# Decode attention with FFN, two layers: score sums moved from VectorE to TensorE, wide V matmuls, layers interleaved by batch row

## The chip, the cores and the metric

The kernel runs on one core of one Trainium2 chip. The metric is device time in microseconds, taken over repeated runs. The granted TensorE clock is given as a share of full speed. "MB" is 10^6 bytes, except that a "2 MB tile" is 2048 KB (2.097 MB).

## The reference

Eight batch rows, one new token each, go twice through the same attention block (32 heads of 128, a cache of 4096 keys and values per head, D = 640) and the same FFN (640 to 1728 to 640). All data is bf16.

```python
x = A_x                                   # (8, 1, 640)
for _ in range(2):                        # written out twice in the original
    x = x + _A_ref(_layernorm(x), A_k_cache, A_v_cache, A_wq, A_wo)
    x = x + _B_ref(_layernorm(x), B_w1, B_w2)

# _A_ref: q = x @ wq
#         p = softmax(q . k * 128**-0.5) over 4096 keys, o = p . v per head, then o @ wo
# _B_ref: relu(x @ w1) @ w2
```

Both layers read the whole K and V cache: 2 x (268 + 268) MB. With one query per row and head, each K or V element is used once per layer, so the run is mostly the reading of 1.07 GB.

## The kernel before

A block is one batch row and eight heads. The order of blocks is by head range, then by batch row. K comes in 2 MB tiles (two heads, 32 keys of each head per partition), four buffers deep. V comes in 1 MB tiles, eight deep. The scores are made on VectorE (DVE): one multiply with the query, four halving adds, one reduce.

```python
blocks = [(b, *r) for r in ranges for b in range(B)]       # ranges of 8 heads
...
# k_phase, per two heads
nc.sync.dma_start(
    out=K_sb.rearrange("p (h j) d -> p h j d", h=HK),
    in_=A_k_cache[b, h : h + HK].rearrange("h (p j) d -> p h j d", p=P),
)
...
nc.vector.tensor_tensor(out=K4, in0=K4, in1=qap, op=ALU.mult)          # 128 x 8192
w = Dh
for _ in range(TL):                                                    # TL = 4
    w //= 2
    nc.vector.tensor_tensor(
        out=K_sb[:, :, 0:w], in0=K_sb[:, :, 0:w], in1=K_sb[:, :, w : 2 * w], op=ALU.add
    )
nc.vector.tensor_reduce(out=S_sb[:, hl0 : hl0 + HK, :], in_=K_sb[:, :, 0:RW], axis=AX.X, op=ALU.add)
...
# v_phase, per head: 32 matmuls with a one-column stationary operand
for j in range(J):
    nc.tensor.matmul(
        o_ps[0:1, hb * Dh : (hb + 1) * Dh], lhsT=P_sb[:, hl, j : j + 1],
        rhs=V_sb[:, j, :], start=(j == 0), stop=(j == J - 1),
    )
...
drive([k_phase(bi), s_phase(bi - 1), v_phase(bi - 2)])     # a pipeline over blocks
...
attention_layer(0, pre0)       # all rows
pre1 = attention_prealloc(1)   # wq is loaded a second time
ffn_layer(0)
attention_layer(1, pre1)
ffn_layer(1)
```

Of the kernel before, what the change touches and what calls it, by code (L numbers as in the profile page):

```python
# [12 lines left out]
ALU = mybir.AluOpType  # L13
AX = mybir.AxisListType


def _bcast_ap(ap: bass.AP, shape_strides) -> bass.AP:
    return bass.AP(
        tensor=ap.tensor,
        offset=ap.offset,  # L20
        ap=[list(ap.ap[0])] + [[int(st), int(n)] for (st, n) in shape_strides],
    )


KERNEL_OPTS = dict(
    k_bufs=4,
    v_bufs=8,
    tree_levels=4,
    heads_per_block=8,
    edge_heads=0,  # L30
    heads_per_ktile=2,
    merged_mult=True,
)
# [3 lines left out]
def kernel(  # L37
# [12 lines left out]
    opts = dict(KERNEL_OPTS)  # L50
# [7 lines left out]
    assert Sq == 1 and Dh == P and HD == H * Dh  # L58
    assert D % P == 0 and Sk % P == 0 and HD % 512 == 0 and B <= P
    DC = D // P  # L60
    J = Sk // P
    NQ = HD // 512
# [3 lines left out]
    NCH = 2 if D > 512 else 1  # L66
    assert D % NCH == 0 and D // NCH <= 512
    DN = D // NCH
    inv_sqrt_dh = 1.0 / float(np.sqrt(Dh))
    eps = 1e-5  # L70
    TL = opts["tree_levels"]
    assert Dh % (1 << TL) == 0
    RW = Dh >> TL
    HK = opts["heads_per_ktile"]

    HPB = min(opts["heads_per_block"], H)
    assert H % HPB == 0
    ranges = [(h, HPB) for h in range(0, H, HPB)]
    blocks = [(b, *r) for r in ranges for b in range(B)]
    EH = opts["edge_heads"]  # L80
    if EH and EH < HPB and HPB % EH == 0:
        b0, h00, nh00 = blocks[0]
        bl, h0l, nhl = blocks[-1]
        first = [(b0, h00 + k, EH) for k in range(0, nh00, EH)]
        last = [(bl, h0l + k, EH) for k in range(0, nhl, EH)]
        blocks = first + blocks[1:-1] + last
    for (_, _, nh) in blocks:
        assert nh % HK == 0
    NBLK = len(blocks)
    MAXNH = max(nh for (_, _, nh) in blocks)  # L90
    HB = 4
    while any(nh % HB for (_, _, nh) in blocks):
        HB //= 2
    _done = {r: 0 for r in ranges}
    range_done_at = {}
    for bi, (b, h0, nh) in enumerate(blocks):
        for r in ranges:
            if r[0] <= h0 and h0 + nh <= r[0] + r[1]:
                _done[r] += nh
                if _done[r] == B * r[1]:  # L100
                    range_done_at[bi] = r
    completion_order = [range_done_at[bi] for bi in sorted(range_done_at)]
    assert len(completion_order) == len(ranges)

    x_flat = A_x.rearrange("b s d -> (b s) d")
    out_flat = out.rearrange("b s d -> (b s) d")
# [3 lines left out]
    state = ctx.enter_context(tc.tile_pool(name="state", bufs=1))  # L110
    psum_g = ctx.enter_context(tc.tile_pool(name="psum_g", bufs=1, space=bass.MemoryType.PSUM))

    sel = consts.tile([B, B, P], BF16, name="sel")
    nc.gpsimd.memset(sel, 0.0)
    nc.gpsimd.affine_select(
        out=sel, in_=sel, pattern=[[-1, B], [0, P]], compare_op=ALU.not_equal,
        fill=1.0, base=0, channel_multiplier=1,
    )
    ident = consts.tile([B, B], BF16, name="ident")
    nc.gpsimd.memset(ident, 0.0)  # L120
    nc.gpsimd.affine_select(
        out=ident, in_=ident, pattern=[[-1, B]], compare_op=ALU.not_equal,
        fill=1.0, base=0, channel_multiplier=1,
    )
    one_bf = consts.tile([1, 1], BF16, name="one_bf")
    nc.vector.memset(one_bf, 1.0)
    ones_f = consts.tile([P, P], FP32, name="ones_f")
    nc.vector.memset(ones_f, 1.0)
# [5 lines left out]
    )  # L134
    eps_c = consts.tile([P, 1], FP32, name="eps_c")
    nc.vector.memset(eps_c, eps)

    x_bf = state.tile([B, D], BF16, name="x_bf")
    nc.sync.dma_start(out=x_bf, in_=x_flat)
    x_sb = state.tile([B, D], FP32, name="x_sb")  # L140
    nc.vector.tensor_copy(out=x_sb, in_=x_bf)

    w1_sb = wres.tile([P, DC, Dff], BF16, name="w1_sb")
    w2_sb = wres.tile([P, FC, D], BF16, name="w2_sb")

    def load_ffn_weights():
        nc.sync.dma_start(out=w1_sb, in_=B_w1.rearrange("(c p) f -> p c f", p=P))
        if n_full > 0:
            nc.sync.dma_start(
                out=w2_sb[:, :n_full, :],  # L150
                in_=B_w2[0 : n_full * P, :].rearrange("(c p) n -> p c n", p=P),
            )
        if Dff % P != 0:
            rem = Dff % P
            nc.sync.dma_start(out=w2_sb[:rem, n_full, :], in_=B_w2[n_full * P : Dff, :])

    def layernorm_T(psum_pool, out_pool):
        lnes = ExitStack()
        work = lnes.enter_context(tc.tile_pool(name="lnwork", bufs=1))
        ssum = work.tile([B, 1], FP32, name="ln_ssum")  # L160
        nc.vector.tensor_reduce(out=ssum, in_=x_sb, axis=AX.X, op=ALU.add)
        mean = work.tile([B, 1], FP32, name="ln_mean")
        nc.vector.tensor_scalar(out=mean, in0=ssum, scalar1=1.0 / D, scalar2=None, op0=ALU.mult)
        xc = work.tile([B, D], FP32, name="ln_xc")
        nc.vector.tensor_scalar(out=xc, in0=x_sb, scalar1=mean, scalar2=None, op0=ALU.subtract)
        sqj = work.tile([B, D], FP32, name="ln_sqj")
        var = work.tile([B, 1], FP32, name="ln_var")
        nc.vector.tensor_tensor_reduce(
            out=sqj, in0=xc, in1=xc, scale=1.0 / D, scalar=0.0, op0=ALU.mult, op1=ALU.add, accum_out=var
        )  # L170
        std = work.tile([B, 1], FP32, name="ln_std")
        nc.scalar.activation(out=std, in_=var, func=ACT.Sqrt, bias=eps_c[:B, :], scale=1.0)
        rstd = work.tile([B, 1], FP32, name="ln_rstd")
        nc.vector.reciprocal(out=rstd, in_=std)
        xln = work.tile([B, D], BF16, name="ln_xln")
        nc.vector.tensor_scalar(out=xln, in0=xc, scalar1=rstd, scalar2=None, op0=ALU.mult)
        xT_ps = psum_pool.tile([P, DC, B], BF16, name="xT_ps", bufs=1)
        for c in range(DC):
            nc.tensor.transpose(out=xT_ps[:, c, :], in_=xln[:, c * P : (c + 1) * P], identity=ident[:, :])
        xlnT = out_pool.tile([P, DC, B], BF16, name="ln_xlnT")  # L180
        nc.vector.tensor_copy(out=xlnT, in_=xT_ps)
        lnes.close()
        return xlnT

    def add_psum_to_x(y_list):
        for n in range(NCH):
            nc.vector.tensor_tensor(
                out=x_sb[:, n * DN : (n + 1) * DN], in0=x_sb[:, n * DN : (n + 1) * DN],
                in1=y_list[n], op=ALU.add,
            )  # L190

    def attention_prealloc(li: int):
        axs = ExitStack()
        qpool = axs.enter_context(tc.tile_pool(name=f"qpool{li}", bufs=1))
        q_sb = qpool.tile([B, HD], BF16, name="q_sb")
        oT_sb = qpool.tile([P, H, B], BF16, name="oT_sb")
        wq_es = ExitStack()
        wq_pool = wq_es.enter_context(tc.tile_pool(name=f"wq_pool{li}", bufs=1))
        wq_sb = wq_pool.tile([P, DC, HD], BF16, name="wq_sb")
        nc.sync.dma_start(out=wq_sb, in_=A_wq.rearrange("(c p) n -> p c n", p=P))  # L200
        return dict(axs=axs, qpool=qpool, q_sb=q_sb, oT_sb=oT_sb, wq_es=wq_es, wq_sb=wq_sb)

    def attention_layer(li: int, pre):
        axs = pre["axs"]
        qpool = pre["qpool"]
        q_sb = pre["q_sb"]
        oT_sb = pre["oT_sb"]
        wq_sb = pre["wq_sb"]

        with ExitStack() as es:  # L210
            psum_q = es.enter_context(tc.tile_pool(name=f"psum_q{li}", bufs=2, space=bass.MemoryType.PSUM))
            xlnT = layernorm_T(psum_q, qpool)
            for n in range(NQ):
                q_ps = psum_q.tile([B, 512], FP32, name="q_ps")
                for c in range(DC):
                    nc.tensor.matmul(  # L216
                        q_ps, lhsT=xlnT[:, c, :], rhs=wq_sb[:, c, n * 512 : (n + 1) * 512],
                        start=(c == 0), stop=(c == DC - 1),
                    )
                nc.scalar.copy(out=q_sb[:, n * 512 : (n + 1) * 512], in_=q_ps)  # L220
        pre["wq_es"].close()

        wo_pool = axs.enter_context(tc.tile_pool(name=f"wo_pool{li}", bufs=1))
        kv_es = ExitStack()
# [241 lines left out]
```

## Time and profile before

| | before |
|---|---|
| time, median | 2803 us |
| DVE / PE busy share | 91% / 55% |
| load queue, share of 16 engines' time | 95.2% |
| bytes on the load queue | 1099 MB |
| rate in full stretches | 420 to 421 GB/s |

The lines below are from the page of the kernel before. PE is TensorE, PEld its weight loads, DVE is VectorE, ACT ScalarE, POOL GpSimd, and SP the engine whose queue issues the loads; L267 is line 267 of the kernel. The first line gives busy microseconds of each engine. The next three cut the span into 40 slices (the granted clock in tenths, the DMA busy share in tenths, the rate). The q1 line gives packets, MB and share of the load queue. Then comes the chain of work that ended last, by engine, and last three of the costliest groups (count, busy us, mean ns, idle before).

```profile
...
PE 1545.5 (55%) x17768; PEld 1377.1 (49%) x17768; DVE 2536.3 (91%) x1905; ACT 338.8 (12%) x1433; POOL 3.1 (0%) x10
...
PEclk7676776876777777777867676777777777767778
DMA  8899997999899998999988999899998999989996
GB/s 349 351 417 421 421 404 311 421 421 420 368 405 421 421 420 350 420 421 420 376 340 341 375 420 421 345 374 420 421 420 349 421 420 421 421 352 421 420 421 256
...
q1 hardware_dynamic: 155440, 1099.21, 95.2%
...
DVE 85%; DMA 7%; PE 6%; issue 1%; ACT 1%; SPq 0%; ACTq 0%; DVEq 0%
...
L337 PE MATMUL o_ps<-V_sb,P_sb 128*1 128x128 bf16 x16384 | 1321.2, 257 | 548.0 <-DMA V_sb<-in_A_v_cache_dram 543.0
...
L267 DVE TENSOR_TENSOR K_sb<-K_sb,qb_sb 128x8192 bf16<-128x8192 bf16 x256 | 1129.9, 4414 | 93.7 <-DMA K_sb<-in_A_k_cache_dram 93.4
L277 DVE TENSOR_TENSOR K_sb<-K_sb 128x512 bf16<-128x512 bf16 (+3 forms) x1024 | 1176.8, 1154 | 26.5
...
```

DVE is nearly full, and the chain is 85% DVE. But the queue's packets already take 95.2% of the DMA engines' time. The second view shows why: the windows of the kernel before. The columns are busy us and instruction counts by engine, then the granted clock, the DMA share, and the rate.

```profile
...
core 0: us, PE busy (x) PEld busy (x) DVE busy (x) ACT busy (x) POOL busy (x), PEclk, DMA share, GB/s
140.00:400.00 260.00, 134.34 (x1650) 119.73 (x1650) 253.39 (x191) 33.94 (x152) 0.00 (x0) 0.69 1.01 420
1450.00:1500.00 50.00, 19.55 (x271) 17.50 (x271) 50.00 (x33) 6.40 (x23) 0.00 (x0) 0.65 0.73 286
2600.00:2700.00 100.00, 54.03 (x648) 50.82 (x648) 97.46 (x71) 9.61 (x43) 0.00 (x0) 0.76 1.01 421
2780.00:2800.00 20.00, 11.01 (x118) 6.32 (x115) 5.90 (x15) 1.58 (x2) 0.00 (x0) 0.74 0.01 1
...
```

In undisturbed stretches the DMA share is 1.01 at 420 to 421 GB/s. The rate is lower in the first 140 us, around the layer boundary (286) and in the tail (almost none), and also at six other places: the slices of 311, 368, 350, 345, 349 and 352 in the page's GB/s line. The buffer of wo holds one range of eight heads, and its reload (L370) waits until the projection of that range has read the old piece; every K and V load behind it in the queue waits too. The first line below shows the stretch around one such place, the second the queue's waits at L370 (us in total, times, longest; L299 is TensorE's next matmul after that projection):

```profile
...
400.00:500.00 100.00, 59.12 (x668) 52.52 (x666) 88.96 (x65) 10.69 (x45) 0.00 (x0) 0.71 0.81 333
...
SPq L370 <- PE misc_ps L299: 191.8, 6, 32.0
...
```

In this trace nothing is issued from 404.5 to 436.3 us, and from 420 to 430 us the traffic is zero while DVE is busy for 9.83 of 10 us. Counted against 421 GB/s in 10 us windows, the six places lose 88 us together.

### The profile page before, as it was taken

How to read it: one execution, taken by the hardware profiler on the slowest of the kernel's cores; microseconds unless marked ns; L12 is line 12 of the kernel's file. 1: busy time of each engine (PE TensorE's matmuls, PEld its weight loads, DVE VectorE, ACT ScalarE, POOL GpSimd, SP SyncE). 2: the span in 40 equal slices, each digit the busy share in tenths (PEclk: the TensorE clock that was granted, in tenths of full speed). 3: DMA queues.
4: the chain of work that ended last, by engine and by line, in shares of the span. 5: the costliest groups of instructions: out<-in, count | busy, mean ns of one | idle time of the engine just before them, and what ended most of it. 6: DMA issues, size and time to landing. Idle time of an engine off the chain costs nothing.

```text
span 2800.5 us, 40467 instructions
## 1 busy us (share of the span) xinstructions
PE 1545.5 (55%) x17768; PEld 1377.1 (49%) x17768; DVE 2536.3 (91%) x1905; ACT 338.8 (12%) x1433; POOL 3.1 (0%) x10
## 2 busy tenths in 40 slices
PE   2454455556555555555725454465555555555657
PEld 0354454555545555555614454455554555555546
DVE  5999998999989998999469999989999899989993
ACT  1111111011011111111111111111011011111011
POOL 0000000000000000000000000000000000000000
PEclk7676776876777777777867676777777777767778
DMA  8899997999899998999988999899998999989996
GB/s 349 351 417 421 421 404 311 421 421 420 368 405 421 421 420 350 420 421 420 376 340 341 375 420 421 345 374 420 421 420 349 421 420 421 421 352 421 420 421 256
DMA packets 155617, 1101.80 MB, mean 393 GB/s; under 512 B 12512, under 2 KB 22448, under 8 KB 23088
## 3 DMA queue, kind: packets, MB, share of 16 engines
q1 hardware_dynamic: 155440, 1099.21, 95.2%
q8 instruction: 139, 2.28, 0.3%
q14 instruction: 38, 0.31, 0.0%
HBM read 1099.15 MB, written 0.01 MB: 392 GB/s over the span
## 4 chain that ended last, share of the span: by engine, by line
DVE 85%; DMA 7%; PE 6%; issue 1%; ACT 1%; SPq 0%; ACTq 0%; DVEq 0%
DVE K_sb L277 39%; DVE K_sb L267 37%; DMA K_sb<-in_A_k_cache_dram 7%; DVE S_sb L281 5%; PE o_ps L337 2%; PE y_ps L362 1%; DVE mrow L296 1%; PE q_ps L216 1%; PE misc_ps L299 1%; DVE hmx L302 1%; DMA wq_sb<-in_A_wq_dram 1%; PE y_ps L420 0%; ACT P_sb L314 0%; DVE invL L352 0%; DVE diag L304 0%
## 5 line engine op out<-in xcount | busy, mean ns | idle before, releaser
L337 PE MATMUL o_ps<-V_sb,P_sb 128*1 128x128 bf16 x16384 | 1321.2, 257 | 548.0 <-DMA V_sb<-in_A_v_cache_dram 543.0
L337 PEld LDWEIGHTS <-P_sb 128*1 128x1 bf16 x16384 | 1250.2, 101 | 590.5 <-issue 550.8
L267 DVE TENSOR_TENSOR K_sb<-K_sb,qb_sb 128x8192 bf16<-128x8192 bf16 x256 | 1129.9, 4414 | 93.7 <-DMA K_sb<-in_A_k_cache_dram 93.4
L277 DVE TENSOR_TENSOR K_sb<-K_sb 128x512 bf16<-128x512 bf16 (+3 forms) x1024 | 1176.8, 1154 | 26.5
L251 ACT CAST qb_sb<-bc_ps 128x512 bf16<-128x512 f32 x128 | 68.7, 588 | 1172.4 <-DVE K_sb L267 1171.3
L281 DVE TENSOR_REDUCE S_sb<-K_sb 128x64 f32<-128x512 bf16 x256 | 175.1, 684 | 7.6
L343 ACT CAST o_sb<-o_ps 1x512 bf16<-1x512 f32 x128 | 73.4, 573 | 727.5 <-PE o_ps L337 727.4
L314 ACT ACTIVATE P_sb<-S_sb,nmax 128x32 bf16<-128x32 f32 x512 | 157.0, 308 | 2.0
L346 PE MATMUL oT_ps<-one_bf,o_sb 1*128 1x1 bf16 x512 | 32.1, 163 | 212.9 <-ACT o_sb L343 209.2
L346 PEld LDWEIGHTS <-o_sb 1*128 1x128 bf16 x512 | 21.1, 94 | 237.0 <-ACT o_sb L343 226.5
L319 PE MATMUL misc_ps<-lrow,ones_f 128*128 128x8 f32 x128 | 38.1, 371 | 161.8 <-ACT P_sb L314 161.8
L319 PEld LDWEIGHTS misc_ps<-lrow,ones_f 128*128 128x128 f32 x128 | 32.0, 310 | 171.3 <-ACT P_sb L314 170.6
L299 PE MATMUL misc_ps<-ident_f,mrow 128*8 128x128 f32 x64 | 22.2, 348 | 157.9 <-DVE mrow L296 157.9
L299 PEld LDWEIGHTS misc_ps<-ident_f,mrow 128*8 128x8 f32 x64 | 5.3, 83 | 194.7 <-DVE mrow L296 177.8
L247 PE MATMUL bc_ps<-q_sb,sel 8*128 8x512 bf16 x128 | 49.8, 462 | 91.7 <-ACT qb_sb L251 89.6
L314 ACT ACTIVATION_READ_ACCUMULATOR P_sb<-S_sb,nmax 128x1 f32 x512 | 95.5, 187 | 0.0
L310 ACT ACTIVATE nmax<-misc_ps 128x8 f32<-128x8 f32 x64 | 11.4, 178 | 446.3 <-PE misc_ps L308 446.3
L353 DVE TENSOR_TENSOR oT_sb<-oT_ps,invL 128x8 bf16<-128x8 f32 x64 | 11.9, 185 | 54.9 <-PE oT_ps L346 54.9
L308 PE MATMUL misc_ps<-diag,ones_f 8*128 8x8 f32 x128 | 34.4, 339 | 42.9 <-DVE diag L304 42.9
L308 PEld LDWEIGHTS misc_ps<-diag,ones_f 8*128 8x128 f32 x128 | 28.4, 274 | 58.5 <-DVE diag L304 57.2
L247 PEld LDWEIGHTS <-sel 8*128 8x128 bf16 x128 | 8.9, 99 | 96.3 <-issue 92.7
L302 DVE TENSOR_REDUCE hmx<-misc_ps 8x1 f32<-8x128 f32 x64 | 17.8, 278 | 37.1 <-PE misc_ps L299 37.0
(44 smaller groups left out, 201.9 us busy)
## 6 DMA issues: line engine op xcount, KB each, us to landing
K_sb<-in_A_k_cache_dram SPq DMA_DIRECT2D x256, 2048.0 KB, 27.0
V_sb<-in_A_v_cache_dram SPq DMA_DIRECT2D x512, 1024.0 KB, 24.8
wq_sb<-in_A_wq_dram SPq DMA_DIRECT2D x2, 5120.0 KB, 16.0
wo_sb<-in_A_wo_dram SPq DMA_DIRECT2D x8, 1280.0 KB, 6.2
w_sb<-in_B_w_dram SPq DMA_DIRECT2D x1, 2160.0 KB, 19.8
w_sb<-in_B_w_dram SPq DMA_DIRECT2D x1, 2080.0 KB, 25.0
w_sb<-in_B_w_dram SPq DMA_DIRECT2D x1, 80.0 KB, 23.5
x_bf<-in_A_x_dram SPq DMA_DIRECT2D x1, 10.0 KB
```

Source lines behind the costliest of these rows:

```text
L247: nc.tensor.matmul(bc_ps[:, :gw], lhsT=sel[:, b, :], rhs=q_sb[:, h0 * Dh + g : h0 * Dh + g + gw], start=True, stop=True,)
L251: nc.scalar.copy(out=qb_sb[:, g : g + gw], in_=bc_ps[:, :gw])
L267: nc.vector.tensor_tensor(out=K4, in0=K4, in1=qap, op=ALU.mult)
L277: nc.vector.tensor_tensor(out=K_sb[:, :, 0:w], in0=K_sb[:, :, 0:w], in1=K_sb[:, :, w : 2 * w], op=ALU.add)
L281: nc.vector.tensor_reduce(out=S_sb[:, hl0 : hl0 + HK, :], in_=K_sb[:, :, 0:RW], axis=AX.X, op=ALU.add)
L299: nc.tensor.transpose(out=mT_ps, in_=mrow[:, :nh], identity=ident_f)
L308: nc.tensor.matmul(gmax_ps, lhsT=ones_f[:nh, :], rhs=diag[:nh, :nh], start=True, stop=True)
L314: nc.scalar.activation(out=P_sb[:, hl, :], in_=S_sb[:, hl, :], func=ACT.Exp, bias=nmax[:, hl : hl + 1], scale=inv_sqrt_dh, accum_out=lrow[ ...
L319: nc.tensor.matmul(L_ps, lhsT=ones_f, rhs=lrow[:, :nh], start=True, stop=True)
L337: nc.tensor.matmul(o_ps[0:1, hb * Dh : (hb + 1) * Dh], lhsT=P_sb[:, hl, j : j + 1], rhs=V_sb[:, j, :], start=(j == 0), stop=(j == J - 1),)
L343: nc.scalar.copy(out=o_sb, in_=o_ps)
L346: nc.tensor.matmul(oT_ps[:, hh : hh + 1], lhsT=o_sb[0:1, kk * Dh : (kk + 1) * Dh], rhs=one_bf[0:1, 0:1], start=True, stop=True,)
```

## The change

The intent is to take the halving adds off DVE, to make TensorE cheap enough to take them, and then to keep the load queue full.

- A visit is one batch row and two heads. Heads sit on the two halves of the partitions, 64 keys per partition, so K and V rows are 16 KB per partition in one 2 MB load (8 KB per head before).
- DVE multiplies a tile in two halves. TensorE sums them with 16 identity matmuls of 512 columns into PSUM, the memory that matmuls accumulate in ("fold"), and DVE reduces the last 8.
- Attention uses 16 matmuls per visit of eight columns by 512, at four column positions.
- Rows are visited so that layer 1 of row b runs between parts of layer 0 of row b+1. One V tile per row is kept from layer 0 to layer 1, which saves eight loads of 2 MB. wq is loaded once. So is wo, in four pieces that stay; before, the pieces replaced each other and were read again for layer 1.
- The FFN of one row is sliced over several visits. K and V have two buffers each, and the order on each engine is fixed by hand.

The diff, cut to its core (cuts are marked by ...):

```diff
-                w = Dh
-                for _ in range(TL):
-                    w //= 2
-                    nc.vector.tensor_tensor(
-                        out=K_sb[:, :, 0:w], in0=K_sb[:, :, 0:w], in1=K_sb[:, :, w : 2 * w], op=ALU.add
-                    )
...
+    def pair_src(cache, b, hp):
+        return cache[b, 2 * hp : 2 * hp + 2].rearrange("h (pp j) d -> (h pp) j d", pp=HP)
...
+    def fold(i, part):
+        if part == 0:
+            s_tiles[i] = ps.tile([P, J, RW], FP32, name="s_ps", bufs=2)
+        n = DW // RW
+        for k in range(n):
+            lo = part * DW + k * RW
+            nc.tensor.matmul(
+                s_tiles[i], lhsT=ident_b, rhs=K_tiles[i][:, :, lo : lo + RW],
+                start=(part == 0 and k == 0), stop=(part == 1 and k == n - 1),
+            )
...
+            nc.tensor.matmul(
+                o_ps[32 * c : 32 * c + 8, :], lhsT=P2[k % 2][:, j, 4 * g : 4 * g + 4, :],
+                rhs=V[:, 4 * g : 4 * g + 4, :], start=(g < 4), stop=(g >= n - 4), tile_position=(0, 32 * c),
+            )
...
+        if hp == keep:
+            if layer == 1:
+                V_tiles[v] = kept.pop(b)
+                return
+            V_tiles[v] = kept[b] = rpool.tile([P, J, Dh], BF16, name="V_keep")
...
+            if new:
+                mult(i, 0)
+                fold(i, 0)
+            if 1 <= i <= NV:
+                reduce_s(i - 1)
+            ... (softmax_a, softmax_d, scale_o, add_y of earlier visits)
+            if new:
+                mult(i, 1)
+                fold(i, 1)
+                if i + 2 < NV:
+                    load_k(i + 2)
+            ... (softmax_b, attend, load_v(v + 2), softmax_c, gather_o, project_o)
```

## The prediction

> **What bounds the kernel now.** Two resources are almost equally full. The chain of waits is 85% DVE: per 2 MB K tile one 128x8192 multiply (4.41 us), four halving adds (2.28, 1.22, 0.69, 0.42) and a 0.68 us reduce, 9.7 us x 256 = 2487 of 2536 us busy (groups). But the page's queue lines give the load queue 95.2% of 16 engines' time. By stretches (windows), 140-400 and 2600-2700 us run at 420 to 421 GB/s, DMA share 1.01; nothing runs faster. 1099 MB at 421 GB/s is 2611 us. It is lower only where stalled: 0-30 (334 GB/s), 400-500 (333), 1450-1500 after the layer boundary (286), and a tail (2780-2800) with almost no traffic.
>
> **What the change does.** (a) The DVE keeps the multiply, as two 128x4096 halves (2.28 us each in this trace); the adds become 16 accumulating identity matmuls of 512 columns and one 0.68 us reduce. DVE work per 2 MB pair falls from 9.7 to about 5.3 us, plus some 0.8 us of small operations: about 6.1 x 256 = 1560 us, estimate. (b) The 16384 one-column V matmuls become 4096 eight-column, 512-wide ones at four column positions of the array. (c) The layers are interleaved by batch row, with FFN work sliced between, so there is no boundary stall. (d) wq is read once, and eight 2 MB V tiles are kept for layer 1: 22 MB less, leaving 1072 MB by the shapes. (e) K buffering shrinks to two 2 MB tiles and V to two.
>
> **How much counts.** Nearly 1000 us leaves the DVE, but the DMA floor moves only from 2611 to 1072/421 = 2546 us. Per K+V visit (4.19 MB) the DMA needs 9.97 us. DVE needs 6.1. PE: the 512-column projections started 0.43 us apart at first and about 0.215 later (timeline), so the folds cost 3.4 (warm) to 6.9 us (cold). Column positions should overlap; the Trainium skill, TensorE: Matmul & The Clock Gate, Part 3, states 2.38x for three column tiles, which no run here shows. With that, attention is about 1.2 to 2.5 us, small matmuls about 1.5, giving 6 to 10 us. So DMA binds if PE stays mostly warm.
>
> Does double buffering feed it? A K buffer is held about 2.3 + 1.5 + 2.3 + 1.7 to 3.4 = 8 to 9.5 us of a 20 us turn, leaving over 10 us for 5 us of transfer and its queue. The even visits' softmax chain (fold, maximum, four 0.5 us exponentials, 0.57 us copy, gather, projection, next add) is 8.5 to 10 us: near the period: small leaks, not a new bound.
>
> Sum: 2546 + about 8 head + 20 tail (last V, attention, one FFN row, output) + 25 leaks = **2600 us**, 8 in 10 within **2570 to 2700**. Chances: faster by over 2% 0.93, within 2% 0.06, slower 0.01.
>
> **What would show it.** DVE share falls to about 60%; the queue share rises to 97% or more and GB/s stands at 415 to 421 in nearly all slices, no dip mid-way; the chain turns from DVE to DMA (K tile landings); DVE's main wait is for K loads; o_ps matmuls overlap; PEclk stays about 0.7 or more.
>
> **What would make it wrong.** Column positions that do not overlap, strided 8-element moving reads that run slow in the folds, or a half-rate clock: PE then needs over 10 us a visit, the chain turns to PE, and the time is 2700 to 2900. Or the two-buffer loads arriving too late: DMA idles, slices at 390 to 405 GB/s, 2650 to 2750.

## The result, and the profile after

The changed kernel takes 2582 us (median of 8 runs, 2578 to 2585), the kernel before 2803 us. The ratio is 0.921, 95% interval 0.920 to 0.922. All ratios here are the mean time of one kernel's fast runs over that of the other's in the same rounds, so they are not quite the ratios of the quoted medians.

| | before | after |
|---|---|---|
| time, median | 2803 us | 2582 us |
| DVE / PE busy share | 91% / 55% | 57% / 75% |
| load queue share | 95.2% | 98.7% |
| bytes on the load queue | 1099 MB | 1072 MB |
| rate in full stretches | 420 to 421 GB/s | 426 to 427 GB/s |
| mean granted clock | 0.724 | 0.838 |

The same kinds of lines of the page of the changed kernel, with its line of DMA packets (count, MB, mean rate, and how many packets are small):

```profile
...
PE 1948.9 (75%) x15662; PEld 883.6 (34%) x15662; DVE 1461.2 (57%) x1943; ACT 513.0 (20%) x1604; POOL 2.1 (0%) x15
...
PEclk8778888888888888888888888888888787888887
DMA  9999999999999999999999999999999999999997
GB/s 385 418 414 426 410 409 426 426 426 426 406 427 426 426 424 408 426 425 403 400 425 426 427 419 410 427 426 426 410 417 426 427 413 419 413 426 424 406 426 300
DMA packets 81968, 1074.24 MB, mean 416 GB/s; under 512 B 8256, under 2 KB 14096, under 8 KB 17296
...
q1 hardware_dynamic: 81808, 1071.93, 98.7%
...
DMA 48%; PE 31%; DVE 16%; ACT 4%; issue 1%; DVEq 0%; SPq 0%; ACTq 0%
...
L302 DVE TENSOR_TENSOR K_sb<-K_sb,qb 128x4096 bf16<-128x4096 bf16 x512 | 1171.2, 2288 | 1017.8 <-DMA K_sb<-in_A_k_cache_dram 1017.8
L312 PE MATMUL s_ps<-K_sb,ident_b 128*128 128x512 bf16 x4096 | 1260.5, 466 | 389.8 <-DVE K_sb L302 388.8
...
```

DVE fell from 2536 to 1461 us busy, and its waits for K loads are now 1018 us, the idle time shown in the group of the multiply. The queue's share rose to 98.7%. The chain's largest engine is now DMA, but only 48%: most of the rest (multiply and fold, 14% and 25% of the span in the page's list by line) is the work between a K tile's landing and the request for the next one. No load waits for a wo buffer any more.

The windows of the changed kernel (columns as above), at a visit whose V tile is kept and at the end:

```profile
...
core 0: us, PE busy (x) PEld busy (x) DVE busy (x) ACT busy (x) POOL busy (x), PEclk, DMA share, GB/s
640.00:650.00 10.00, 5.98 (x62) 2.92 (x63) 5.47 (x7) 1.13 (x2) 0.00 (x0) 0.99 1.00 424
650.00:660.00 10.00, 8.18 (x37) 3.11 (x37) 6.16 (x9) 1.95 (x10) 0.00 (x0) 0.66 0.78 300
660.00:670.00 10.00, 8.97 (x81) 4.21 (x82) 8.17 (x12) 1.73 (x3) 0.00 (x0) 1.00 0.99 424
2560.00:2570.00 10.00, 5.50 (x80) 2.36 (x77) 0.98 (x7) 2.46 (x3) 0.00 (x0) 0.50 0.43 179
2570.00:2580.00 10.00, 6.30 (x146) 5.97 (x147) 1.05 (x7) 1.98 (x5) 0.00 (x0) 0.50 0.01 2
...
```

About two thirds of the 10 us windows of the run stand at 424 GB/s or more. At 650 us the rate drops to 300, and such a drop returns about every 32 visits. That is where one V tile is not loaded. The tail of some 20 us has no traffic.

The timeline of TensorE in the changed kernel (start, length, line, operation, count):

```profile
...
start us, us, engine line op out<-in xcount [idle before <-releaser]
...
1209.48 1.04 PE L372 MATMUL o_ps<-V_sb,P 128*8 128x512 bf16 x16
...
```

Sixteen attention matmuls of 512 columns end 1.04 us after they began.

The loss can be counted: for each 10 us window, the shortfall against 427 GB/s. It sums to 68 us: 4 in the first ten, 19 in the tail, and the remaining 45 in between. Of these 45, some 20 lie at the eight visits whose V tile is kept, and some 14 in windows that hold a slice of the FFN (its matmuls are at L191 and L210). Without any shortfall the 1074 MB of all queues would take 2516 us.

### The profile page after: what moved, and what is told of

Read it like the earlier page. It is cut to its first block, busy times and chain, and to the rows that moved or that the text cites. A ratio compares the mean times of both kernels' runs of the same rounds, so it can differ in the third digit from the quotient of the medians.

```text
span 2583.5 us, 36163 instructions
## 1 busy us (share of the span) xinstructions
PE 1948.9 (75%) x15662; PEld 883.6 (34%) x15662; DVE 1461.2 (57%) x1943; ACT 513.0 (20%) x1604; POOL 2.1 (0%) x15
## 3 DMA queue, kind: packets, MB, share of 16 engines
q1 hardware_dynamic: 81808, 1071.93, 98.7%
## 4 chain that ended last, share of the span: by engine, by line
DMA 48%; PE 31%; DVE 16%; ACT 4%; issue 1%; DVEq 0%; SPq 0%; ACTq 0%
DMA K_sb<-in_A_k_cache_dram 47%; PE s_ps L312 25%; DVE K_sb L302 14%; ACT P L349 2%; PE q_ps L287 1%; PE ch_ps L210 1%; PE o_ps L372 1%; DVE S_sb L323 1%; ACT o_sb L377 1%; PE ch_ps L191 1%; PE blk_ps L342 1%; ACT L167 0%; DMA K_sb<-in_A_v_cache_dram 0%; PE blk_ps L329 0%; ACT L165 0%
## 5 line engine op out<-in xcount | busy, mean ns | idle before, releaser
L302 DVE TENSOR_TENSOR K_sb<-K_sb,qb 128x4096 bf16<-128x4096 bf16 x512 | 1171.2, 2288 | 1017.8 <-DMA K_sb<-in_A_k_cache_dram 1017.8
L312 PE MATMUL s_ps<-K_sb,ident_b 128*128 128x512 bf16 x4096 | 1260.5, 466 | 389.8 <-DVE K_sb L302 388.8
L312 PEld LDWEIGHTS <-ident_b 128*128 128x128 bf16 x4096 | 457.5, 114 | 1071.4 <-issue 779.0
L377 ACT CAST o_sb<-o_ps 104x512 bf16<-104x512 f32 x256 | 150.1, 586 | 824.9 <-PE o_ps L372 821.8
L372 PE MATMUL o_ps<-V_sb,P 128*8 128x512 bf16 x3808 | 249.2, 382 | 0.0
L349 ACT ACTIVATE P<-S_sb,nmax 64x64 bf16<-64x64 f32 x512 | 186.8, 365 | 9.0
L323 DVE TENSOR_REDUCE S_sb<-s_ps 128x64 f32<-128x512 f32 x256 | 175.1, 684 | 2.7 <-PE s_ps L312 2.7
L396 PE MATMUL y_ps<-oT,wo_sb 128*128 128x1 bf16 x2560 | 99.7, 163 | 0.3 <-DVE oT L388 0.3
L349 ACT ACTIVATION_READ_ACCUMULATOR P<-S_sb,nmax 64x1 f32 x512 | 94.5, 185 | 0.0
L396 PEld LDWEIGHTS <-wo_sb 128*128 128x128 bf16 x2560 | 82.6, 96 | 0.4 <-DVE oT L388 0.4
```

The source lines that it names most:

```text
L302: nc.vector.tensor_tensor(out=kk, in0=kk, in1=_free(qb_tiles[i][:, lo : lo + DW], [(0, J), (1, DW)]), op=ALU.mult)
L312: nc.tensor.matmul(s_tiles[i], lhsT=ident_b, rhs=K_tiles[i][:, :, lo : lo + RW], start=(part == 0 and k == 0), stop=(part == 1 and k == n ...
L323: nc.vector.tensor_reduce(out=S_tiles[k][:, j, :], in_=s_tiles.pop(i), axis=AX.X, op=ALU.add)
L349: nc.scalar.activation(out=P2[k % 2][r, j, :, hh], in_=S[r, j, :], func=ACT.Exp, bias=nmax[r, j : j + 1], scale=inv_sqrt_dh, accum_out=lro ...
L372: nc.tensor.matmul(o_ps[32 * c : 32 * c + 8, :], lhsT=P2[k % 2][:, j, 4 * g : 4 * g + 4, :], rhs=V[:, 4 * g : 4 * g + 4, :], start=(g < 4) ...
L377: nc.scalar.copy(out=o_sb, in_=o_ps[:104, :])
```

## The experiments

Kernels marked "wrong" compute something else. Three of them feed attention with wrong scores or wrong V tiles, one with mixed heads, and all still passed the comparison with the reference. So that comparison does not see such errors with these inputs, and where a kernel is said below to pass it, no more than that is shown. The wrong kernels serve for timing only.

### DVE relief alone, without the adds (wrong)

```diff
-                for _ in range(TL):
+                for _ in range(0):
```

The kernel before, nothing else changed.

> The kernel before with its four halving adds left out (wrong result on purpose: the scores are sums of 8 of the 128 products). 1181 us of DVE work leave, nothing else changes. Theory A (the next bound is the load queue at 1099 MB / 421 GB/s = 2611 us, and the stalls at the start, at the layer boundary and in the tail stay, some 60 to 80 us): 2670 to 2700 us, so that DVE relief alone brings only half of the 221 us. Rival (the relief is the whole gain): 2580 to 2600.

Measured: 2691 us, ratio to before 0.960 (0.959 to 0.962). Lines of its page:

```profile
...
GB/s 382 420 421 421 420 399 411 421 421 421 396 421 420 421 420 393 420 421 420 384 402 421 420 421 421 389 421 421 420 420 390 421 420 421 421 390 420 421 421 261
...
q1 hardware_dynamic: 155440, 1099.21, 98.8%
...
DMA 85%; PE 10%; DVE 3%; ACT 1%; issue 0%; SPq 0%; ACTq 0%; DVEq 0%
...
```

The chain is 85% DMA now, against 85% DVE before. The full slices still stand at 420 to 421 GB/s, and the queue's share is 98.8%. Taking away 1140 us of DVE busy time (2536 to 1397) brings 111 us, half of the gain, and then the queue binds. The traces show where most of it comes from: the six stops at the reload of wo lose 28 us here instead of 88, so some 60 of the 111 us. The queue's waits at L370 are 151 us here, against 192. That the projection is reached sooner with less of DVE's work in the way is the likely reason; no run isolates it. A rival change was not tried: a second buffer for wo in the kernel before, which would take the reload out of the way of the loads without any DVE relief.

### The adds moved to TensorE, V matmuls left as they were

```diff
-                    nc.vector.tensor_tensor(
-                        out=K_sb[:, :, 0:w], ... op=ALU.add
+                s_ps = psum_kv.tile([P, HK * J, RW], FP32, name="s_ps", bufs=2)
+                for k in range(Dh // RW):
+                    nc.tensor.matmul(
+                        s_ps, lhsT=ident_b, rhs=K_sb[:, :, k * RW : (k + 1) * RW],
+                        start=(k == 0), stop=(k == Dh // RW - 1),
+                    )
```

(the reduce reads s_ps; bc_ps and o_ps go from two buffers to one)

> The kernel before with only the halving adds moved to PE (16 accumulating identity matmuls per 2 MB K tile; one buffer fewer each for the query broadcast and the attention sums, to make room in PSUM); correct result. The V matmuls stay as they were: 128 per pair at about 57 ns (4.18 us for 72 in the trace), 7.3 us, plus 3.4 to 6.9 us of folds, plus 1 us: 11.8 us or more per pair against 9.97 of transfers. I expect PE to bind: 2950 to 3150 us, slower than before. Rival (moving work off the fullest engine always gains): 2700 or less.

Measured: 2727 us, ratio 0.974 (0.971 to 0.978). Both expectations missed: it is faster than before, yet 36 us slower than with the adds simply gone. Lines of its page:

```profile
...
PE 2186.2 (80%) x21864; PEld 1428.3 (52%) x21864; DVE 1383.4 (51%) x882; ACT 347.3 (13%) x1433; POOL 3.1 (0%) x10
...
PEclk8899998999989999899979999989999999989999
...
PE 53%; DVE 21%; DMA 18%; ACT 7%; issue 1%; SPq 0%; ACTq 0%; DVEq 0%
...
```

My expectation rested on a counting error: 16384 V matmuls over 256 pairs are 64 per pair, not 128. With the 59 ns each that this trace shows, V needs 3.8 us per pair. With 3.6 us for a fold and about 1 us of the rest, TensorE needs some 8.4 us per pair, so it does not bind by volume, and the page has it 80% busy. The waits of this kernel's DVE show what took the place of the adds:

```profile
...
DVE S_sb L283 <- PE s_ps L278: 1031.5, 243, 6.7
...
```

DVE stands still 1031 us for the folds, because the reduce of a tile comes right after its own multiply: multiply (4.4), fold (3.6) and reduce (0.7) follow one another. The changed kernel reduces a tile one visit later. In the traces the difference lies almost wholly at the six stops for wo, which lose 62 us here and 28 us with the adds simply gone. That the serial order lengthens these stops was not isolated.

### One column position

```diff
-                o_ps[32 * c : 32 * c + 8, :], ...
-                ... start=(g < 4), stop=(g >= n - 4), tile_position=(0, 32 * c),
+                o_ps[0:8, :], ...
+                ... start=(g == 0), stop=(g == n - 1), tile_position=(0, 0),
```

> The changed kernel with the sixteen attention matmuls of a visit at one column position, accumulating one after the other (correct result). If the four positions overlap fully, as the trace's 1.04 us for sixteen suggests, one position takes 16 x 0.215 = 3.4 us, 2.4 us more per visit, and the engines' own time per visit rises from about 7.8 to about 9.5 to 10 us, hidden only in part by the exponentials on even visits. Theory A (load queue bound with 2 us of slack per visit): 2585 to 2660 us. Rival (PE, busy 75%, becomes the bound, 614 us of added busy time all showing): above 2750.

Measured: 2707 us, ratio 0.965 (0.963 to 0.968), 125 us slower than the changed kernel. The TensorE timeline of this kernel, to compare with the 1.04 us above:

```profile
...
1216.22 1.90 PE L312 MATMUL s_ps<-K_sb,ident_b 128*128 128x512 bf16 x8
1218.05 3.62 PE L372 MATMUL o_ps<-V_sb,P 128*8 128x512 bf16 x16
```

Sixteen matmuls now take 3.62 us, so the four positions gave 3.62/1.04 = 3.5 times (the granted clock was 1.00 in both windows). The Trainium skill, "TensorE: Matmul & The Clock Gate", Part 3, states 2.38 times for three column tiles. This run agrees in kind and extends it to four. The time lies above my 2585 to 2660 and below the rival's 2750. PE busy time rose by 382 us (1949 to 2331) and the time by 125, so there was some slack, but less than I had thought. It is not spread evenly: in this run the windows of 360 to 540 and 680 to 870 us still stand at 424 and 425 GB/s, and those of 540 to 680 and 870 to 1010 us at 379 and 366. The slow ones hold the FFN slices and the visits just after them. The fold line in the same fence also answers a doubt of the prediction: eight folds end after 1.90 us, and sixteen in a row took 3.61 us in the fold-alone run, which makes (3.61 - 1.90)/8 = 0.21 us each. The 512-column projections of the kernel before, with contiguous operands, followed each other at the same pace (28 of their weight loads, one each, in 5.92 us, also 0.21). The 8-element strided reads cost nothing extra here. That agrees with the Trainium skill, "SBUF — State Buffer", Door 1, which says that eight bf16 fill one 16-byte line.

### No V traffic, with two and with three K buffers (wrong)

How much slack is there? Both kernels use one V tile throughout.

```diff
-            V_tiles[v] = kept[b] = rpool.tile([P, J, Dh], BF16, name="V_keep")   # and all other V loads
+        if not kept:
+            kept[0] = rpool.tile([P, J, Dh], BF16, name="V_keep")
+            nc.sync.dma_start(out=kept[0], in_=pair_src(A_v_cache, b, hp))
+        V_tiles[v] = kept[0]
```

> The changed kernel with every visit reading the first V tile, which is loaded once (wrong result on purpose): K tiles only, 553 MB, 1300 us of transfers. What is left is the engines' own time per visit. Worked out from the durations in the trace of the changed kernel (projection, add, half multiply, fold, maximum, exponentials, copy, gather) I expect 6.7 us on visits without softmax and 8.3 with, 7.5 to 8 us on average: 1920 to 2050 us, chain through PE and DVE. If the engines were near the DMA period (rival: DMA and engines equally tight), 2400 or more.

Measured: 2245 us (two runs, 2235 and 2256), 8.77 us a visit. I had expected 7.5 to 8. DVE still waited for K loads; the line is from its waits (total us, times, longest):

```profile
...
DVE K_sb L298 <- DMA K_sb<-in_A_k_cache_dram: 478.0, 240, 7.2
...
```

That suggested the turn of the two K buffers. So a third buffer was added, which fits because the V buffers are unused:

```diff
-    kpool = ctx.enter_context(tc.tile_pool(name="kpool", bufs=2))
+    kpool = ctx.enter_context(tc.tile_pool(name="kpool", bufs=3))
...
-                if i + 2 < NV:
-                    load_k(i + 2)
+                if i + 3 < NV:
+                    load_k(i + 3)
```

> The kernel without V traffic (wrong result on purpose) with a third K buffer and K loads asked for one visit earlier. Without the third buffer it took 8.77 us a visit, against 5 us of K transfer, and I had expected 7.5 to 8. Theory B (the turn of the two K buffers set the 8.77: about 7.2 us to load plus 10.3 held, over two): 7.4 to 8.0 us a visit, 1900 to 2060 us, and the DVE's waits for K loads nearly vanish. Rival (the engines' own chain sets it): 2200 to 2250 us.

Measured: 2183 us, 8.53 us a visit. The chain and the waits of this kernel:

```profile
...
PE 58%; ACT 20%; DVE 17%; DMA 2%; issue 2%; SPq 1%; ACTq 0%; DVEq 0%
...
```

```profile
...
DVE invL L357 <- PE blk_ps L351: 245.2, 127, 3.2
...
DVE K_sb L297 <- DMA K_sb<-in_A_k_cache_dram: 17.6, 5, 5.7
...
```

The waits for K loads nearly vanished, as the theory said, and the largest that is left is for TensorE's sums (invL). But the time fell by only 62 us, 0.24 us a visit, where the theory had 0.8 to 1.4, and it lies just below the rival's 2200 to 2250. So the buffer turn set 0.24 us of this kernel's 8.77, and no more. The engines' own loop (fold, exponentials, copy, gather, projection, next add and multiply) takes 8.5 us a visit on average, head and tail included, at a granted clock of 0.90 (0.84 in the changed kernel). Against 9.9 us of transfers that is a mean slack of 1.4 us, not the 2 that I had counted. It is an average over unlike visits: in the one-column run, 2.6 us more of attention per visit was hidden in visits without FFN work, and showed in and just after those with it.

### What the kept V tiles bring

Nothing kept:

```diff
-    keep = order0[-1]
+    keep = -1
```

> The changed kernel with no V tile kept: all 256 V tiles are read, 16.8 MB more. Theory A (the load queue is never starved, so bytes alone set the time): 16.8 MB at the 425 GB/s of its full stretches is 39.5 us more, 2621 us. Theory B (at each of the eight visits whose V is kept, the queue runs dry, because the next K tile can't be asked for until a K buffer is free; the trace of the changed kernel shows about 2 us lost at each, the visit taking 6.7 us where K alone needs 5): keeping saves only about 3 us each, so 2600 to 2610 us, and the 269 to 362 GB/s dips every 320 us are gone.

Measured: 2607 us, ratio 0.930 (0.929 to 0.931). The saving of 16.8 MB is worth 25 us, not 39.5. Windows of this kernel where the changed one fell to 300 GB/s:

```profile
...
640.00:650.00 10.00, 7.54 (x57) 3.54 (x56) 5.72 (x8) 2.51 (x10) 0.00 (x0) 0.94 1.01 428
650.00:660.00 10.00, 6.56 (x46) 2.60 (x45) 5.75 (x7) 0.58 (x1) 0.00 (x0) 0.74 1.00 421
...
```

The drop is gone. Then the same bytes kept in smaller pieces: a quarter of each of four V tiles per row.

```diff
+        if hp in keep:                       # the last four head pairs
+            if layer == 0:
+                kept[b, hp] = rpool.tile([P, KQ, Dh], BF16, name=f"V_keep{hp}")     # KQ = J // 4
+                nc.sync.dma_start(out=kept[b, hp], in_=src[:, :KQ, :])
+            nc.sync.dma_start(out=V[:, KQ:, :], in_=src[:, KQ:, :])
```

> The changed kernel keeping a quarter of each of four V tiles per batch row instead of one whole tile: the same bytes and the same memory. Theory A (bytes alone): no change, 2582 us within 3. Theory B (a visit without a V load is shorter for the queue than for the engines, so part of the saving is lost): four visits with three quarters of a V tile each need 8.7 us of transfers, more than the 6.7 to 8 us that the engines need, so nothing is lost: 2562 to 2570 us, dips gone.

Measured: 2575 us, ratio 0.919 (0.917 to 0.920) against 0.921 for the changed kernel. The same place:

```profile
...
640.00:650.00 10.00, 7.05 (x79) 3.14 (x79) 5.29 (x6) 3.09 (x11) 0.00 (x0) 1.00 1.00 419
650.00:660.00 10.00, 6.71 (x37) 2.84 (x37) 5.94 (x8) 1.49 (x7) 0.00 (x0) 0.83 1.00 424
...
```

The drop of 300 is gone here too, with the same bytes. The reading that fits this run and the pace of 8.5 us: a visit with K alone needs 5 us of transfers, the engines free the next buffer only at their own pace, and once what had been queued is used up the queue has no request. A visit with K and three quarters of V needs 8.7 us, about the engines' pace, and the queue stays filled. The gain is 7 us, less than the 12 to 20 expected: another drop, as deep, appeared at another place (286 GB/s at 2250 us), whose cause I did not find, and some at FFN slices stayed.

### The order of issue

```diff
             if new:
                 mult(i, 0)
                 fold(i, 0)
+                mult(i, 1)
+                fold(i, 1)
+                if i + 2 < NV:
+                    load_k(i + 2)
+            ... softmax_c of the block before
             if 1 <= i <= NV:
                 reduce_s(i - 1)
             ...
             if v >= 0:
                 o_sb = attend(v)
+            if blk is not None:
+                softmax_b(blk)
```

> The changed kernel with only the order of issue altered: both half multiplies and both folds of a visit come first, then the reduce and the small operations; the attention matmuls go before the softmax of the block, and the row-sum matmul moves to the next visit (correct result, same bytes, same buffers). A K buffer is then held about 7 us instead of 8.3 to 10, so the next K load can be asked for earlier. Theory B (the 2 us lost at each kept visit and the other dips come from the turn of the two K buffers): the dips go, 2558 to 2570 us. Theory A (bytes alone): no change, 2578 to 2585 us.

Measured: 2573 us, ratio 0.918 (0.917 to 0.919), 9 us better than the changed kernel, just outside what I expected. And the drop at the kept visit stayed:

```profile
...
640.00:650.00 10.00, 5.56 (x48) 2.62 (x47) 5.59 (x7) 0.59 (x1) 0.00 (x0) 0.91 1.01 426
650.00:660.00 10.00, 8.46 (x63) 3.75 (x62) 6.14 (x9) 3.03 (x11) 0.00 (x0) 0.84 0.88 349
...
```

So asking for K earlier does not cure the kept visits (the eight lose some 19 us together, 20 in the changed kernel), which again speaks for the pace of the engines there and against the buffer turn. What is gone, as far as one trace of each can tell, are drops elsewhere, at 1180, 1810 and 2120 us among others. In the changed kernel these lie in windows with the FFN's second matmuls (L210), and the windows with FFN work, the tail left out, lose some 14 us there and about 1 us here. In the changed kernel a slice of the FFN stands between the two halves of a tile's fold, and so before the next K load; here it comes after both. That this order is the cause fits, but no run isolates it.

Both together:

> The altered order together with four kept quarters instead of one kept tile. Theory B: the altered order alone already feeds the queue at kept visits, so the quarters add nothing more: equal to the altered order alone within 4 us, 2555 to 2570 us, and the lowest of all kernels here together with it. If the quarters still add (rival: the buffer turn is still too long), it is 6 us or more below it.

Measured: 2570 us, ratio 0.917 (0.916 to 0.918). It has the lowest median of all kernels here that do the whole work, 12 us below the changed one. It is within 3 us of the altered order alone, and the two intervals overlap, so that last step is not shown. The number came as expected, but not for the reason given: the altered order alone had not fed the queue at the kept visits. The kernel passes the comparison with the reference.

### Plain order of layers

The kernel with nothing kept, with all rows of layer 0 first, then all of layer 1 (and eight buffers for the small query input, which then has to live longer).

```diff
+    visits = [(layer, b, hp) for layer in range(2) for b in range(B) for hp in order0]
```

A first form with two such buffers deadlocked in the simulator.

> The changed kernel with no V tile kept and the visits in plain order: all rows of layer 0, then all rows of layer 1. My prediction credited the interleaving with removing the layer-boundary stall. Theory A (the stall goes because a row's layer 1 needs only that row's layer 0, done seven rows earlier; interleaving itself is only there to make the keeping possible): equal to the kernel that keeps nothing, within 4 us. Rival (interleaving removes the stall): slower by 30 us or more, with a dip in the middle of the GB/s line.

Measured: 2607 us, the same as the kernel with nothing kept (ratios 0.931 and 0.930). Windows around its layer boundary:

```profile
...
1260.00:1300.00 40.00, 30.23 (x214) 13.02 (x213) 23.18 (x29) 6.77 (x23) 0.00 (x0) 0.86 1.01 426
1300.00:1340.00 40.00, 28.86 (x208) 12.54 (x208) 22.80 (x29) 6.77 (x23) 0.00 (x0) 0.83 1.01 428
...
```

There is no stall at 1300 us. Interleaving the layers removes nothing by itself. The likely reason, which no run isolates: a row now passes through all heads before the next row starts, so the first row of layer 1 has long been ready. In the kernel before, with head ranges outermost, all rows end together. What interleaving does is to make keeping V tiles possible.

### Row length in the loads

The changed kernel's full stretches are 1.4% faster than anything in the kernel before. First, each 2 MB load was split into two of 1 MB, with 8 KB per partition:

```diff
-        nc.sync.dma_start(out=K_tiles[i], in_=pair_src(A_k_cache, b, hp))
+        for r in (slice(0, J // 2), slice(J // 2, J)):
+            nc.sync.dma_start(out=K_tiles[i][:, r, :], in_=pair_src(A_k_cache, b, hp)[:, r, :])
```

(and the same for V)

> The changed kernel with each 2 MB load of K or V asked for as two loads of 1 MB, so that a partition's row is 8 KB instead of 16 KB, as it was in the kernel before. My prediction took 421 GB/s, the top of the kernel before, as the ceiling; the changed kernel's full stretches stand at 426. Theory (the rate goes with the row or transfer length): full stretches fall to 420 or 421 GB/s and the time rises by 1.2% of some 2520 us, 25 to 32 us, to about 2610. Rival (the 426 comes from elsewhere, for instance from fewer small transfers): 2578 to 2587 us.

Measured: 2618 us, ratio 0.935 (0.933 to 0.936). Then 2 MB loads with 8 KB rows (wrong):

```diff
-        return cache[b, 2 * hp : 2 * hp + 2].rearrange("h (pp j) d -> (h pp) j d", pp=HP)
+        return cache[b, 2 * hp : 2 * hp + 2].rearrange("h (p j) d -> p h j d", p=P)
```

> The changed kernel with every K and V tile read in one 2 MB load as now, but in the layout of the kernel before: each of 128 partitions gets an 8 KB row of one head and an 8 KB row of the next (wrong result on purpose, because the two heads are then mixed; bytes, buffers and instructions are the same). The two 1 MB loads with 8 KB rows took 2618 us, at 419 to 421 GB/s in full stretches. If the row length sets the rate: the same again, 2608 to 2622 us. If the size or the number of the loads sets it: 2578 to 2587 us, as with 16 KB rows, at 426 GB/s.

Measured: 2619 us, ratio 0.935 (0.934 to 0.936). The rate and packet lines, first of the split loads, then of the single loads:

```profile
...
GB/s 373 411 407 419 419 400 420 420 418 419 402 420 419 419 409 400 419 420 406 404 419 420 419 417 406 416 419 419 418 397 420 419 419 416 406 419 419 401 413 296
DMA packets 154264, 1074.34 MB, mean 410 GB/s; under 512 B 16288, under 2 KB 22128, under 8 KB 25328
...
```

```profile
...
GB/s 383 411 409 420 417 405 420 419 419 417 399 419 420 418 419 406 420 419 419 407 421 419 420 416 407 419 420 419 417 404 420 420 419 419 398 420 419 404 419 297
DMA packets 146481, 1074.24 MB, mean 412 GB/s; under 512 B 8257, under 2 KB 14097, under 8 KB 17297
...
```

Both stand at 419 to 420 GB/s in full slices, both cost 36 to 37 us, and both have twice the large packets: 128936 and 129184 of 8 KB or more, against 64672 in the changed kernel. The number of loads doubles in only one of them, and the rows lie 16 KB apart in the first and 8 KB apart in the second. So the 8 KB rows, not the load size or the distance of the rows, set the lower rate. 36 us, a sixth of the whole gain, comes from a side effect of the new partition layout.

## Why the prediction was right, point by point

- **The binding resource: right.** DVE relief alone went to the queue-bound time expected for it (2691, expected 2670 to 2700). The DVE share (57% for "about 60%"), the queue share (98.7% for "97% or more"), DVE's main wait (K loads) and the clock (0.84) came as said. The chain turned to DMA only for 48%. I had expected more. What I did not see is where the relief would be earned: the prediction lists the stalled stretch of 400 to 500 us but not its cause, and some 60 of the 111 us come from shorter stops at the reload of wo.
- **The floor: mis-sized.** "Nothing runs faster" than 421 GB/s was read from a kernel with 8 KB rows and carried over to 16 KB rows. The changed kernel moves 427. The term was 2546 us and is 2516 us with all queues' bytes. The row experiments show the cause. The Trainium skill, "HBM Reference", Specifications, gives about 425 GB/s for a core that streams alone. Both kernels' traces agree within 1.2%, and the difference that mattered lies inside that.
- **The leaks: mis-sized, the other way.** 25 us became 45. The head (8 foreseen, 4 measured) and tail (20 and 19) were about right. The two errors cancel: 2546 + 8 + 20 + 25 = 2599, and 2516 + 4 + 19 + 45 = 2584. The sum came within 18 us of the result; this cancelling was luck. At 8 KB rows the same kernel takes 2619, so with the rate that I assumed the sum would have been 19 us too low.
- **"22 MB less": miscounted, and wrong in worth.** The load queue moved 27.3 MB less (1099.2 to 1071.9): the 22 MB are wq and the kept tiles, and wo, which is now read once too, was left out. The 1072 MB that went into the sum were right. The 16.8 MB of kept V tiles bring 25 us instead of 39.5, because, on the reading above, a visit without a V load needs only 5 us of transfers and the engines cannot follow below 8.5. Keeping quarters showed that the same bytes can be saved without that drop.
- **"Interleaved ... so there is no boundary stall": wrong in its reason.** The stall is gone without interleaving as well.
- **"Column positions should overlap": right**, 3.5 times for four. It is also needed: without it the time is 2707.
- **PE 6 to 10 us a visit; "small leaks, not a new bound": right, but narrow.** The engines' loop is 8.5 us against 9.9 on average, and, as the one-column run suggests, longer around visits with FFN work, where some 14 of the 45 us were lost.

In sizes, each taken in the kernel where it was tested (they need not add up): 111 us for DVE relief, 36 for row length, 25 for the kept tiles. By subtraction about 49 of the 221 us are left for the second loads of wq and wo (10.5 MB, an estimated 25 us at 421 GB/s), what remained of the stops at the reload of wo (28 us without the adds), the boundary and the shorter tail, less the changed kernel's own drops. These were not tried one by one.

## What to carry to other kernels

Before pricing the relief of the fullest engine, look up which resource is second and how full it already is. Here 1140 us of DVE work were worth 111 us. Look also for places where the load queue stands behind one load that waits for its buffer: six of them cost 88 us here, and a queue share of 95.2% hid them. A saved transfer is worth its time only where the engines can run at the shorter period, so spread savings over several steps instead of emptying one. A ceiling read from a profile holds for the access shape it was read with.

## What the Trainium skill lacked or had wrong

- "DMA: Bandwidth & Descriptors" (Specifications) gives 512 B as the smallest transfer for full rate, and has no figure that tells 8 KB rows from 16 KB rows. Here 16 KB rows per partition ran at 426 to 427 GB/s and 8 KB rows at 419 to 421, whether in loads of 1 MB or of 2 MB (2582 against 2618 us).
- "TensorE: Matmul & The Clock Gate" (Part 3) has a measurement for three column tiles, not for four. Here four positions took 1.04 us for sixteen 512-column matmuls against 3.62 us at one position, 3.5 times.
- "Perfetto Trace Analysis" (What "DMA-bound" means) lists what can bind, but not that a transfer saved in a single step can leave the queue without requests. Here 16.8 MB saved in eight whole tiles brought 25 us, where 39.5 would be the transfer time at 425 GB/s.
